# Attention and SoLU block on one core: the first two batches in slots of two pairs, v loaded once, q in halves

## The chip, the cores and the metric

The kernel runs on one core of a Trainium2 chip. Its engines are named as in the profile: PE (TensorE matmul) with PEld (its weight loads), DVE (VectorE), ACT (ScalarE), POOL (GpSimd) and SP (SyncE, which here only issues DMAs). The metric is the device time of one execution in microseconds (us); less is better.

## What is computed

The reference has two blocks. Batch is 8, heads 8, sequence 576, head width 64; the second block is 512 to 1024 to 512 wide.

```python
def _attn_ref(q, k, v, tau):
    scale = 1.0 / np.sqrt(q.shape[-1])
    scores = scale * np.matmul(q, k.transpose(0, 1, 3, 2))
    thresh = np.max(scores, axis=-1, keepdims=True) - tau
    scores = np.where(scores >= thresh, scores, -1000000000.0)
    scores = scores - np.max(scores, axis=-1, keepdims=True)
    attn = np.exp(scores)
    attn = attn / (np.sum(attn, axis=-1, keepdims=True) + 1e-09)
    return np.matmul(attn, v).astype(np.float32)

def _moe_ref(x, w_in, w_out, g_ln):
    h = x @ w_in
    h_max = np.max(h, axis=-1, keepdims=True)
    e = np.exp(h - h_max)
    sm = e / (np.sum(e, axis=-1, keepdims=True) + 1e-09)
    solu = h * sm
    mu = np.mean(solu, axis=-1, keepdims=True)
    var = np.mean((solu - mu) ** 2, axis=-1, keepdims=True)
    ln = (solu - mu) / np.sqrt(var + 1e-06) * g_ln
    return (ln @ w_out).astype(np.float32)
```

The heads of a token are laid side by side between the two blocks. All activations are float32. The weights `w_in`, `w_out` and `g_ln` come as float64, and the kernel converts them itself with integer operations on 16 pieces of 128 x 512, 512 KB each (`raw`).

## The kernel before

**Rounds.** The heads of a batch form four pairs. A slot is one step of attention for 128 queries: the scores against all 576 keys, for two heads side by side in two PSUM buffers (`s0`, `s1`). Two slots (r = 0 and 1) make a unit, and a unit is what one PV multiplication takes. Of a batch's 18 slots, kinds 0 and 1 have four units each (one for each pair), and kind 2 has the last 64 queries of all heads (the "ends"). The main loop runs 144 rounds, a slot in each. In a round: `scores` (L492, 16 matmul records on PE), the row maximum on DVE (`maxes`, L514), threshold and exponential on ACT (`ramp` L529, `exps` L538), then for the slot of the round before the division on POOL (`normalise`, L545 to L548) and a 32 x 32 block transpose on DVE (`blocks`, L559) into `T`. After a unit's second slot `spread` issues three DMAs on SP (L580, L582; L589 for ends), which put T's blocks in place in `wT`. When a unit's time has come (`pv_due`), `attend_steps` multiplies wT by v (L619, 72 matmuls) into a PSUM buffer `pv`, and `attended` has ACT copy it to `xh` or `xe` (L652), the input of the second block.

**Before round 30** (`START`) the kernel also fills itself: the pairs of batch 0 and 1 are loaded, turned and evicted, the weights are converted, and four blocks of the second block (`fronts`) are run at rounds that a table fixes: `ff_h` (L1041), a chain on DVE, ACT and POOL up to V (L1124) and its turn (L1157), `ff_o` (L1175) into PSUM `o_ps`, `ff_out` (ACT copies it to `ob`, L1195), `ff_store`. From round 30 on the matmuls of the second block go into two PSUM buffers that are held for good (`both["h"]`, `both["o"]`), and a PV shares the buffer of o. Before round 30 a PV takes one of two pair buffers (`p0`, `p1`) of its own.

**q, k and v of the first two batches.** `load_pair` (L132) brings the first 512 rows of two heads of q or k in one DMA of 256 KB; partition p gets the four rows 4p to 4p+3. `load_ends` (L143) brings the last 64 rows. PE turns them with matmuls against the identity (`turn`, L360), ACT and DVE copy the turned pieces out of PSUM into qT, kT and qe (`q_item` L396 and L400, `k_item` L420, `e_item` L435 and L439), either as `items` of a round's `scores` (batch 1, table PREP) or by `whole_pair`. Before the loop `turned` turns k of pair 0 and a quarter of its q; round 0 turns the other three quarters; whole pairs 1, 2 and 3 come at rounds 0, 2 and 4. A unit here is one pair with both slots, so v has to lie in two orders of its rows: `load_v` (L174, L179) loads, for half a batch (four heads), all 512 rows in 512 KB, then the same rows again with the two partition halves swapped in 2 x 256 KB, then the last 64 rows twice (2 x 64 KB).

**Queues.** SP's queue runs in order and carries the loads, the spreads, most raw pieces and the stores. The first three raw pieces (`weight_load`, L267) are issued by ACT's queue, as are k of pair 0 and tau. A piece goes to one of four work buffers (table RAW) and may be loaded when the piece before it in that buffer has been read. An instruction is issued in the order in which the program names it on its engine; what is not ready holds up all that is behind it on that engine.

**Tables.** PIECE says when each weight piece is loaded and converted (in quarters of a round), FETCH when a load of batch 1 and of v is issued, PREP when a piece of batch 1 is turned, HO in which rounds before 30 the four fronts are multiplied, LAG how much later than its least age a unit's PV is due. In `loose` rounds (19, 28, 29 here: no front, after round 16) DVE copies the scores out with the maximum, so that PSUM comes free earlier.

Of the kernel before, what the change touches and what calls it, by code (L numbers as in the profile page):

```python
# [8 lines left out]
F32 = mybir.dt.float32  # L9
# [11 lines left out]
def kernel(  # L21
# [35 lines left out]
    NB = S // 32  # L57
    SCALE = -0.125
# [67 lines left out]
    def load_pair(i, nm, queue=None):  # L126
        b, hp = divmod(i, NP)
        src = {"q": q, "k": k}[nm]
        raw = raw_tile(nm)[:, 0 : 8 * D].rearrange("p (h t d) -> p h t d", h=2, t=4)
        qk[nm, i] = raw  # L130
        queue = queue or nc.sync
        queue.dma_start(  # L132
            out=raw.rearrange("p h t d -> p h (t d)"),
            in_=src[b, 2 * hp : 2 * hp + 2, 0:SM, :].rearrange("h (p t) d -> p h (t d)", t=4),
        )
        if hp == 0:
            if b not in ends:
                ends[b] = loads.tile([P, H, D], F32, tag="ends", name="ends")
            load_ends(b, nm, slice(0, 2) if b == 0 else slice(0, H), queue)

    def load_ends(b, nm, of, queue):
# [3 lines left out]
        )  # L145

    def load_v(b, hf, parts=(0, 1, 2)):
# [19 lines left out]
        if 0 in parts:  # L167
            d["v"] = loads.tile([P, 4, NK, D], F32, tag="v", bufs=3, name="v")
# [47 lines left out]
    def constants():  # L216
# [4 lines left out]
        for g in range(2):  # L221
            of = 64 + 32 * (1 - g)
            nc.gpsimd.tensor_copy(
                out=swapped[ROWS[1], 32 * g : 32 * g + 32], in_=ident[ROWS[1], of : of + 32]
            )
# [33 lines left out]
    raws = {}  # L259

    def weight_load(x):
        raw = work.tile(
            [P, 512], I64 if wide else F32, tag=("u1", "u2", "uT", "xh1")[RAW[x]],
            bufs=1, name="raw"
        )
# [8 lines left out]

# [79 lines left out]
    def turn(spare, x, lhsT_of, swap=False):  # L354
# [3 lines left out]
        for r in range(2):  # L358
            for y in range(2):
                nc.tensor.matmul(  # L360
                    out=spare[r][ROWS[y], to], lhsT=lhsT_of(r, y),
                    rhs=swapped[ROWS[1]] if swap and r else ident[ROWS[r], ROWS[r]],
# [21 lines left out]
    def q_item(i, ts=slice(0, 4)):  # L384
        qT = pair(i)["qT"].rearrange("p (t r k) -> p r t k", t=4, r=2)
        n = ts.stop - ts.start

        def make(spare, x):
            for t in range(n):
                turn(  # L390
                    spare, x + t, lambda r, y: qk["q", i][ROWS[r], y, ts.start + t], swap=True
# [54 lines left out]
    def whole_pair(i):  # L446
        tags, tiles = zip(take("tp"), take("tp"))
        spare = dict(enumerate(tiles), base=0, eased=i > 0)
# [20 lines left out]

    def scores(s, items):  # L470
# [10 lines left out]
        for ks in (slice(SM, S), slice(0, SM)):  # L481
            for h in range(2):
                for y in range(2):
                    if kind < 2:
# [4 lines left out]
                    else:  # L489
                        d = pairs[b * NP + r + 2 * y]  # L490
# [100 lines left out]
    def attend_steps(key):  # L591
# [13 lines left out]
        for e in range(2) if kind == 2 else [None]:  # L605
            for m in range(NK):
                for u in range(2):
                    d, h0 = source(b * NP + (hp if e is None else e + 2 * u))
                    for h in range(2):
# [4 lines left out]
                        else:  # L614
# [8 lines left out]
                                m ^ 4 * u if m < 8 and b < 2 else m,  # L623
# [7 lines left out]
    def attended(key):  # L631
# [7 lines left out]
        if kind == 2:  # L639
            if b % 2 == 0:  # L640
                xe[b // 2] = work.tile([P, NP, P], F32, tag="xe", bufs=1, name="xe")
            to = xe[b // 2][:, :, 64 * (b % 2) : 64 * (b % 2) + 64].rearrange(
                "p (u r) y -> p u r y", u=2
# [939 lines left out]
```

## Time and profile before

| | us |
|---|---|
| three runs | 849.86, 847.30, 849.82 |
| median | 849.82 |
| the profiled execution | 846.98 |
| its span, first to last instruction | 845.0 |
| PE busy | 799.7 (95%) |
| DVE busy | 671.5 (79%) |
| ACT busy | 604.4 (72%) |
| POOL busy | 565.2 (67%) |
| mean granted clock of PE | 0.981 |

The span is 1.98 us shorter than the execution's own time: what lies around it is not seen in the trace. Busy shares are averages over the whole span. The page's row of the span in 40 slices (each digit is tenths of a slice of 21 us; a 9 is 90% or more) shows where the engines are not busy:

```profile
PE   4769899999899999999999999999999999999997
PEclk9679999999999999999999999999999999999999
DMA  7999688887877868887788768887788767555122
```

PE is under 80% busy in the first three slices (0 to 63 us) alone, the clock granted to it is low in the second and third, and the DMA engines are at 90% or more in slices two to four. The first two batches fill rounds 0 to 35; round 31 begins at 178.57 us.

### The profile page before, as it was taken

Reading aid. Unit: us, or ns where it says so; the run is one execution under the profiler, and the core shown is the slowest. Engines: PE = TensorE matmul, PEld = TensorE weight load, DVE = VectorE, ACT = ScalarE, POOL = GpSimd, SP = SyncE. Lnnn points to the kernel's source line nnn. Section 1 sums busy time; section 2 is a strip of 40 time slices with the busy share of each in tenths; the row PEclk is TensorE's granted clock in tenths of the full one; section 3 lists DMA queues with packets and bytes.
Section 4 is the critical chain, followed back from the end, with each engine's and each line's share of the span. In section 5 each row is a group of like instructions: output and inputs, shape, how many; then the busy total and the mean of one; then the engine's idle time right before and its main releaser. Section 6 shows DMA issues by size and latency. Waiting matters only on the chain.

```text
span 845.0 us, 36864 instructions
## 1 busy us (share of the span) xinstructions
PE 799.7 (95%) x15345; PEld 589.3 (70%) x15345; DVE 671.5 (79%) x1324; ACT 604.4 (72%) x1214; POOL 565.2 (67%) x1031
## 2 busy tenths in 40 slices
PE   4769899999899999999999999999999999999997
PEld 3435567767566886777776677767786677788786
DVE  3888968867889878888889888888888888787362
ACT  5979977676777777778787777878787687876231
POOL 3976867866757758585867758585867758574330
PEclk9679999999999999999999999999999999999999
DMA  7999688887877868887788768887788767555122
GB/s 231 272 231 259 181 221 225 213 220 191 222 224 208 228 149 240 229 216 207 204 244 223 204 163 246 225 221 196 216 238 218 207 159 211 144 152 137 37 62 52
DMA packets 100535, 167.44 MB, mean 198 GB/s; under 512 B 18248, under 2 KB 47952, under 8 KB 100368
## 3 DMA queue, kind: packets, MB, share of 16 engines
q1 hardware_dynamic: 99040, 162.82, 72.3%
q8 instruction: 121, 1.98, 1.0%
q10 hardware_dynamic: 1328, 2.26, 0.9%
q14 instruction: 46, 0.38, 0.1%
HBM read 46.14 MB, written 9.44 MB: 66 GB/s over the span
## 4 chain that ended last, share of the span: by engine, by line
PE 75%; ACT 7%; DMA 5%; POOL 4%; DVE 4%; issue 3%; SPq 2%; DVEq 0%; ACTq 0%; POOLq 0%
PE ov L1175 19%; PE h L735 16%; PE s_ps L492 14%; PE ov L619 12%; PE o_ps L1175 6%; PE h L759 4%; DMA wT<-T 3%; ACT w L529 2%; ACT w L538 2%; PE h_ps L1041 2%; DVE w L514 2%; PE pv L619 2%; POOL w L548 1%; DMA raw<-in_moe_w_out_dram 1%; DMA q<-in_q_dram 1%
## 5 line engine op out<-in xcount | busy, mean ns | idle before, releaser
L529 ACT ACTIVATE w<-s_ps,nth 128x576 f32<-128x576 f32 x282 | 199.6, 741 | 128.5 <-DVE nth L514 113.8
L514 DVE CUSTOM_DVE_ANT_0 w<-s_ps,tau_t 128x576 f32<-128x576 f32 x282 | 201.0, 749 | 55.0 <-PE s_ps L492 36.8
L548 POOL TENSOR_SCALAR w<-w,sm 128x576 f32<-128x576 f32 x288 | 219.0, 772 | 14.3
L559 DVE STREAM_TRANSPOSE T<-w 128x576 f32<-128x576 f32 x288 | 207.7, 756 | 17.8 <-POOL w L548 13.8
L538 ACT ACTIVATE w<-w,ntau 128x576 f32<-128x576 f32 x288 | 219.7, 768 | 0.0
L1175 PE MATMUL ov<-w,uT 64*64 64x256 f32 x3456 | 208.0, 376 | 0.7 <-issue 0.7
L492 PE MATMUL s_ps<-kT,qT 64*64 64x64 f32 (+1 forms) x2048 | 175.4, 424 | 15.1 <-ACT w L529 12.5
L619 PEld LDWEIGHTS ov<-wT,v 64*64 64x64 f32 x4752 | 150.6, 133 | 46.9 <-issue 33.6
L1175 PEld LDWEIGHTS ov<-w,uT 64*64 64x64 f32 x3456 | 160.6, 133 | 26.2 <-issue 1.2
L619 PE MATMUL ov<-wT,v 64*64 64x128 f32 (+1 forms) x4752 | 153.6, 259 | 1.2 <-DMA wT<-T 0.7
L545 POOL TENSOR_SCALAR sm<-sm 128x2 f32<-128x2 f32 x144 | 35.1, 244 | 143.5 <-ACT w L538 138.2
L546 POOL TENSOR_TENSOR sm<-sm,mone 128x2 f32<-128x2 f32 x144 | 104.1, 723 | 12.0
L735 PE MATMUL h<-w,xh 64*64 64x512 f32 x832 | 104.7, 591 | 0.6 <-POOL mark L110 0.4
L492 PEld LDWEIGHTS s_ps<-kT,qT 64*64 64x64 f32 x2048 | 71.4, 139 | 42.3 <-ACT w L529 19.1
L1175 PE MATMUL o_ps<-w,uT 64*64 64x256 f32 x1088 | 66.4, 377 | 0.7 <-ACT xh L652 0.5
L735 PEld LDWEIGHTS h<-w,xh 64*64 64x64 f32 x832 | 43.9, 133 | 31.4 <-issue 20.4
L1175 PEld LDWEIGHTS o_ps<-w,uT 64*64 64x64 f32 x1088 | 57.5, 133 | 10.8 <-issue 4.0
L1130 DVE TENSOR_SCALAR u<-u,rs,nb 128x1024 f32<-128x1024 f32 x32 | 28.8, 900 | 43.4 <-ACT V L1124 43.3
L1157 DVE STREAM_TRANSPOSE uT<-V 128x1024 f32<-128x1024 f32 x36 | 44.3, 1229 | 17.1 <-PE ov L1175 6.9
L538 ACT ACTIVATION_READ_ACCUMULATOR w<-w,ntau 128x1 f32 x288 | 55.7, 193 | 0.0
L735 PE MATMUL h<-k,sum 64*64 64x512 f32 x312 | 51.8, 589 | 0.0
L1124 ACT ACTIVATE V<-u,nb,rs 128x1024 f32<-128x1024 f32 x36 | 44.6, 1238 | 6.5 <-POOL nb L1102 6.4
(132 smaller groups left out, 1015.9 us busy)
## 6 DMA issues: line engine op xcount, KB each, us to landing
wT<-T SPq DMA_DIRECT2D x132, 288.0 KB, 4.5
wT<-T SPq DMA_DIRECT2D x256, 144.0 KB, 3.9
out_dram<-ob SPq DMA_DIRECT2D x71, 128.0 KB, 2.5
V<-u SPq DMA_DIRECT2D x136, 64.0 KB, 2.3
wT<-T SPq DMA_DIRECT2D x14, 576.0 KB, 6.4
q<-in_q_dram SPq DMA_DIRECT2D x24, 288.0 KB, 3.8
q<-in_k_dram SPq DMA_DIRECT2D x24, 288.0 KB, 4.3
v<-in_v_dram SPq DMA_DIRECT2D x12, 576.0 KB, 5.3
```

What stands on the lines that cost most here:

```text
L492: nc.tensor.matmul(out=ps[h][ROWS[y], ks], lhsT=lhsT, rhs=d["kT"][ROWS[h], ks], start=True, stop=True,)
L514: nc.vector.tensor_tensor_reduce(out=w, in0=ps[:, 0:S], in1=(zero if loose else tau_t).to_broadcast([P, S]), scale=1.0, scalar=BIG, op0=AL ...
L529: nc.scalar.activation(out=d["w"][x], in_=d["w"][x] if d["loose"] else d["ps"][x][:, 0:S], func=AF.Prelu, bias=d["nth"][x], scale=-1.0, al ...
L538: nc.scalar.activation(out=w, in_=w, func=AF.Exp, bias=ntau, scale=1.0, accum_out=sm[:, x : x + 1])
L546: nc.gpsimd.tensor_tensor(out=sm, in0=sm, in1=mone, op=ALU.pow)
L548: nc.gpsimd.tensor_scalar(out=w, in0=w, scalar1=sm[:, x : x + 1], scalar2=1.0, op0=ALU.mult, op1=ALU.mult)
L559: nc.vector.transpose(out=T[:, :, r, :, h, :], in_=w.rearrange("p (c m x) -> p c m x", c=2, x=32))
L619: nc.tensor.matmul(out=to, lhsT=d["v"][ROWS[u], (h0 + h - u) % 4 if b > 1 else h0 + h, m ^ 4 * u if m < 8 and b < 2 else m,], rhs=rhs, sta ...
L735: mm = nc.tensor.matmul(out=h[ROWS[y], 512 * bank : 512 * bank + 512], lhsT=x[ROWS[r], ROWS[y]], rhs=w[ROWS[r]], start=c == 0 and (n, r, k ...
L1124: nc.scalar.activation(out=V, in_=u, func=AF.Identity, bias=nb, scale=rs)
L1157: nc.vector.transpose(out=uT, in_=d["V"].rearrange("p y (m x) -> p m y x", x=32))
L1175: nc.tensor.matmul(out=to[ROWS[z], 0:256], lhsT=d["uT"][ROWS[r], m].rearrange("p y x -> p (y x)"), rhs=w2[ROWS[r], m ^ r, 256 * z : 256 * ...
```

## The change

Only the first two batches (`TILED` = 2) and the rounds before 30 are touched.

- **Slots of 64 queries of two pairs.** A slot takes 64 queries of each of two pairs instead of 128 queries of one. A unit is then a couple of pairs j (0: pairs 0 and 1; 1: pairs 2 and 3) and a half m of a kind's 256 queries; with MAJOR all 1 the order is (j, m) = (0,0), (0,1), (1,0), (1,1). Pairs 0 and 1 are both needed at round 0, pairs 2 and 3 at round 4 (before: pair 1 at round 2, pair 2 at 4, pair 3 at 6).
- **v once.** Each half of PE's rows takes another pair of heads, so one order of v is enough. Per half batch `load_v` issues four DMAs of 131 KB and two of 32 KB; one buffer holds a batch.
- **q in halves.** q of pairs 0 and 1 is loaded as two DMAs each (rows 4p, 4p+1 and 4p+2, 4p+3), the second ones behind the first raw piece. Before the loop k, a quarter of q and the ends of both pairs are turned (96 matmuls where 48 were); round 0 turns the second quarter of both, round 1 (LATE) the other half as items of its scores.
- **Whole pairs** 2 and 3 at rounds 1 and 3 (WHEN). The load of q of pair 3 moves from round 0 to the end of round 1.
- **Raw pieces.** The first three go over SP (QUEUE all 0). `weight_load` can put a piece into one of two v buffers (`stash`), for RAW values of 4 and more; the table RAW is as before.
- **o's buffer from round 17** (SHARE): `both["o"]` is taken at round 17, and a PV from there on goes into it, unless a front's o part stands in it unread. `ff_out` gives it back. PVs of the units that end with rounds 15, 17, 19, 21, 23, 25 run in rounds 18, 20, 22, 24, 27, 29 (before: 19, 20, 24, 25, 28, 29).
- PREP of one item of batch 1 moves from round 22 to 21; two more POOL copies fill the second half of `swapped` (the identity with its two 32-blocks exchanged), which q of odd pairs is turned with.

```diff
+    TILED = 2
...
+    def values(b, hf):
+        d = halves.setdefault((b, hf), {})
+        if "v" not in d:
+            if b < TILED:
+                both = loads.tile([P, 4, NK, D], F32, tag="v", bufs=3, name="v")
+                for x in range(2):
+                    halves[b, x] = dict(v=both[:, 2 * x : 2 * x + 2])
+            else:
+                d["v"] = loads.tile([P, 4, NK, D], F32, tag="v", bufs=3, name="v")
+        return halves[b, hf]["v"]
+
+    def stashed():
+        cols = 2 * NK * D if w_in.dtype == I64 else 4 * NK * D
+        return loads.tile([P, cols], w_in.dtype, tag="v", bufs=3, name="stash")
...
+        if b < TILED:
+            for u, rows in enumerate(ROWS):
+                of = v[b, 4 * hf + 2 * u : 4 * hf + 2 * u + 2]
+                to = d["v"][rows, 0:2].rearrange("p h m d -> p h (m d)")
+                for r in range(2) if 0 in parts else ():
+                    part = slice(256 * r, 256 * r + 256)
+                    nc.sync.dma_start(
+                        out=to[:, :, part],
+                        in_=of[:, part].rearrange("h (p t) d -> p h (t d)", t=4),
+                    )
+                if 2 in parts:
+                    nc.sync.dma_start(
+                        out=to[:, :, 512:], in_=of[:, SM:S].rearrange("h p d -> p h d")
+                    )
+            return
...
     def whole_pair(i):
         tags, tiles = zip(take("tp"), take("tp"))
-        spare = dict(enumerate(tiles), base=0, eased=i > 0)
+        spare = dict(enumerate(tiles), base=0, eased=bool(PAIRED[i]))
...
+    def unit_at(b, kind, n):
+        return divmod(n, 2) if MAJOR[2 * b + kind] else divmod(n, 2)[::-1]
...
-                    if kind < 2:
+                    if kind < 2 and b < TILED:
+                        j, m = unit_at(b, kind, hp)
+                        d = pairs[b * NP + 2 * j + y]
+                        t = P * (2 * kind + m) + 64 * r
+                        lhsT = d["qT"][ROWS[h], t : t + 64]
...
-    QUEUE = {0: 1, 1: 1, 2: 1, 3: 0, 4: 0, 5: 0, 6: 0, 7: 0, 8: 0, 9: 0, 10: 0, 11: 0, 12: 0, 13: 0, 14: 0, 15: 0}
...
+    LATE = {0: 1}
+    MAJOR = {0: 1, 1: 1, 2: 1, 3: 1}
+    PAIRED = {2: 1, 3: 1}
+    SHARE = {0: 17}
...
-    load_at = {}
+    load_at = {LATE[0]: [lambda: load_pair(3, "q")]}
...
+        stash = [stashed()]
+        values(0, 0)
+        stash.append(stashed())
+        load_pair(0, "q", ts=slice(0, 2))
+        load_pair(0, "k", nc.scalar)
         nc.scalar.dma_start(out=tau_t, in_=tau.partition_broadcast(P))
-        load_pair(0, "q")
-        load_pair(1, "q")
-        load_pair(0, "k", nc.scalar)
         load_pair(1, "k")
+        load_pair(1, "q", ts=slice(0, 2))
+        constants()
         weight_load(0)
-        constants()
+        for i in range(2):
+            load_pair(i, "q", ts=slice(2, 4))
         for x in range(1, 3):
             weight_load(x)
...
-        turned(first, [k_item(0), q_item(0, slice(0, 1)), e_item(0)])
-
-
-        whole = {0: 1, 2: 2, 4: 3}
...
+        turned(
+            first,
+            [k_item(0), q_item(0, slice(0, 1)), k_item(1), q_item(1, slice(0, 1)), e_item(0), e_item(1)],
+        )
...
             if rnd == START:
-                both["h"], both["o"] = take("h2")[1], take("ov")[1]
+                both["h"] = take("h2")[1]
                 oq.extend(t for x, t in enumerate(fronts) if HO.get(4 * x + 2, START) >= START)
+            if rnd == SHARE[0]:
+                both["o"] = take("ov")[1]
...
-                if due and "o" not in what and len(pairs_free) > ("h" in what and steps[0][1] == 0):
+                opened = both.get("open")
+                for kind, part, _ in steps:
+                    if kind == "o":
+                        opened = None if part else "fresh"
+                if due and opened != "used" and (
+                    "o" in both or len(pairs_free) > ("h" in "".join(x for x, _, _ in steps) and steps[0][1] == 0)
+                ):
```

163 lines of the change are left out of this document (119 added, 44 removed).

## The prediction

> **What bounds the kernel now.** I read the stretches of the span first, because the change touches only the first two batches (36 of 144 rounds) and an average over the span hides them. The columns are the stretch, its length, then busy time and instructions of PE, PEld, DVE, ACT and POOL, the granted clock of PE, the share of the DMA engines, GB/s.
>
> ```profile
> 0.00:18.00 18.00, 8.81 (x176) 5.55 (x176) 5.17 (x17) 7.74 (x20) 3.58 (x16) 1.00 0.81 249
> 18.00:70.00 52.00, 34.69 (x591) 22.57 (x595) 42.41 (x83) 41.87 (x92) 40.02 (x52) 0.74 0.99 240
> 50.00:60.00 10.00, 3.36 (x20) 1.11 (x20) 6.87 (x15) 7.96 (x18) 8.19 (x13) 0.60 1.05 234
> 70.00:104.00 34.00, 30.03 (x592) 20.54 (x584) 30.80 (x60) 32.25 (x69) 29.53 (x42) 1.00 0.82 222
> 104.00:176.00 72.00, 65.84 (x1381) 49.46 (x1381) 55.99 (x109) 51.74 (x112) 55.40 (x94) 0.98 0.86 219
> 176.00:845.00 669.00, 660.37 (x12620) 491.19 (x12612) 537.17 (x1060) 470.78 (x924) 436.67 (x830) 1.00 0.71 190
> ```
>
> From 176 us (round 31) on, PE is busy 660.37 of 669 us, and there the changed program issues the same instructions in the same order: nothing can be won or lost. From 18 to 70 us the DMA engines are full (0.99) and everything else has gaps; from 70 to 176 us PE is close to full (30.03 of 34, 65.84 of 72). So the question is what the change does to 18 to 70 us, and what of it reaches round 31.
>
> What the full DMA engines carry there, and how long one transfer needs from issue to landing (size, median us), against the median of the span in the last row:
>
> ```profile
> wT<-T SPq DMA_DIRECT2D x9, 288.0 KB, 10.3
> ...
> v<-in_v_dram SPq DMA_DIRECT2D x2, 512.0 KB
> v<-in_v_dram SPq DMA_DIRECT2D x4, 256.0 KB, 10.1
> v<-in_v_dram SPq DMA_DIRECT2D x4, 64.0 KB, 9.7
> q<-in_q_dram SPq DMA_DIRECT2D x1, 256.0 KB, 10.8
> ...
> wT<-T SPq DMA_DIRECT2D x132, 288.0 KB, 4.5
> ```
>
> Where it hurts is seen in ACT's waits of 20 to 70 us (the first row) and in the timeline (start, length, what; in brackets the idle time before and what ended it):
>
> ```profile
> ACT xh L652 <- PE pv L619: 5.0, 1, 5.0
> ...
> 43.07 1.42 ACT L529 ACTIVATE w<-s_ps,nth 128x576 f32<-128x576 f32 x2 [1.90 <-DVE nth L514]
> 56.41 1.42 ACT L529 ACTIVATE w<-s_ps,nth 128x576 f32<-128x576 f32 x2 [1.17 <-DVE nth L514]
> 60.18 3.89 PE L619 MATMUL pv<-wT,v 64*64 64x128 f32 x66 [0.45 <-DMA wT<-T]
> 60.26 1.44 DVE L559 STREAM_TRANSPOSE T<-w 128x576 f32<-128x576 f32 x2 [3.26 <-DMA wT<-T]
> 64.33 0.37 ACT L652 COPY xh<-pv 128x256 f32<-128x256 f32 x1 [4.99 <-PE pv L619]
> 66.75 1.42 ACT L529 ACTIVATE w<-s_ps,nth 128x576 f32<-128x576 f32 x2 [0.94 <-DVE nth L514]
> ```
>
> The third unit's spread wT came late, so PV started at 60.18 us, at half clock (3.89 us), and ACT, whose queue runs in order, stood 4.99 us before the copy of that PV and 0.94 us before the next ramp: round 10 starts 5.93 us later than ACT's own work asks.
>
> **The change, part by part.** *The start.* Before, ACT's queue is held by the issues of two raw pieces, and its share of the first evictions follows them; DVE begins its share at 7.13 us.
>
> ```profile
> 5.38 3.60 ACTq L267 DMA_DIRECT2D raw<-in_moe_w_in_dram  x2
> 5.49 1.13 PE L360 MATMUL tp<-ident,k 64*64 64x64 f32 x32 [5.49 <-DMA k<-in_k_dram]
> 7.13 0.42 DVE L420 COPY kT<-tp 128x256 f32<-128x256 f32 x1 [2.20 <-PE tp L360]
> 9.03 0.37 ACT L420 COPY kT<-tp 128x256 f32<-128x256 f32 x1 [4.38 <-DMA q<-in_q_dram]
> 9.50 0.32 ACT L435 ACTIVATE qe<-tp,scl 128x64 f32<-128x64 f32 x1
> 9.67 2.20 PE L492 MATMUL s_ps<-kT,qT 64*64 64x64 f32 x16 [2.62 <-ACT qT L396]
> ```
>
> With the raw pieces on SP, ACT is free at 7.1 us, about 2 us earlier. But round 0 now needs two pairs: 96 transposes for 48 (the second row's 32 of k, and 16 of q and ends), which at 1.13 us for 32 is 1.7 us more of PE, six evictions for three (ACT's three ran 9.03 to 9.82, so 0.8 us more), and pair 1's k must have landed. That is -2 + 1.7 + 0.8, less some overlap: +0.3 us; bounds -1 (transposes under the transfers) and +2.5 (no overlap at all).
>
> *Rounds 1 to 5.* One whole pair's evictions cost ACT 1.7 us:
>
> ```profile
> 24.99 0.82 ACT L396 ACTIVATE qT<-tp,scl 128x256 f32<-128x256 f32 x2
> 25.70 0.64 ACT L420 COPY kT<-tp 128x256 f32<-128x256 f32 x2
> 26.22 0.35 ACT L435 ACTIVATE qe<-tp,scl 128x64 f32<-128x64 f32 x1
> 26.43 0.24 ACT L439 COPY kT<-tp 128x64 f32<-128x64 f32 x1
> ```
>
> By round 4 there were three (pairs 1, 2, 3), now two: -1.7. Four evictions of the late q halves stand between round 1's ramps: each half the 0.82/2 row and its fixed part, +1.1 together; their 32 transposes stand ahead of round 1's scores, +1.3 with the wait behind them. Round 4 now needs pair 3, which is turned in round 3 and was needed only in round 6: its scores wait for ACT's 1.7 us, +1.8. With the start, 0.3 - 1.7 + 1.1 + 1.3 + 1.8 = +2.8 us at round 5. In rounds 6 to 9 ACT waits for DVE's maximum anyway (1.90 us before the ramp at 43.07, 1.17 before the one at 56.41, 3.1 together); I let half of the 2.8 vanish there: +1.4; bounds 0 (the 3.1 take it all) and +2.8.
>
> *v loaded once.* The three v rows are 2 x 512 + 4 x 256 + 4 x 64 KB, 2.36 MB; now half, 1.18 MB. In a full stretch at 240 GB/s that frees 4.9 us of transfer ahead of the wT at 60 us. The wait it feeds is 5.93 us. The next limit is DVE, which has weight steps to do before round 10's maximum; I leave 1.4 us of idle: -4.5. Bounds: -5.9 and 0.
>
> Against this part speaks a rule of the Trainium skill ("DMA: Bandwidth & Descriptors", section Bandwidth): batch transfers, since those under 64 KB are dominated by their descriptors, and 64 KB ran at 138 GB/s there. v now comes in 131 and 32 KB pieces. Worked out with that figure as an estimate, 1.18 MB would take 8.6 us against 9.8 for the 2.36 MB at 240 GB/s, and the part would be worth -1.2 in place of -4.9. The rows lean neither way: 64 KB landed in 9.7 us and 256 KB in 10.1, which in a full queue is mostly waiting in line. The trace cannot settle it; the third rival carries it.
>
> *PV in o's buffer from round 17.* The PV of the eighth unit runs one round earlier, in round 18, and its copy stands in ACT's order ahead of what follows here:
>
> ```profile
> 114.78 1.24 ACT L1124 ACTIVATE V<-u,nb,rs 128x1024 f32<-128x1024 f32 x1 [1.15 <-POOL nb L1102]
> 114.88 2.15 PE L619 MATMUL pv<-wT,v 64*64 64x128 f32 x72
> 115.93 0.57 ACT L1195 COPY ob<-o_ps 128x512 f32<-128x512 f32 x1
> 116.39 0.77 ACT L420 COPY kT<-s_ps 128x192 f32<-128x192 f32 x4
> 116.86 0.76 DVE L514 CUSTOM_DVE_ANT_0 w<-s_ps,zero 128x576 f32<-128x576 f32 x1 [2.85 <-ACT kT L420]
> ```
>
> DVE already waits 2.85 us for that kT. PV and its copy push it by 2.15 + 0.37, less the 1.15 that V waits for POOL anyway: +1.3; bounds 0 and +2.5. Up to round 28 the rounds carry one PV more than before (2.15 us in a PE-bound stretch), and later ones carry it less. A wait there gives some of it back:
>
> ```profile
> 169.86 0.56 ACT L1195 COPY ob<-o_ps 128x512 f32<-128x512 f32 x1
> 170.48 3.21 PE L619 MATMUL pv<-wT,v 64*64 64x128 f32 x72 [2.88 <-ACT ob L1195]
> ```
>
> The 2.88 us before round 29's PV stays, since that PV still follows ACT's ob in the same buffer; I count half of the 2.15 as returned: +1.0; bounds -1 and +2.2.
>
> *Second batch's v.* Another 1.18 MB less, while the DMA share is 0.86 and PE is busy 65.84 of 72 us: -1.0; bounds -2.5 and 0.
>
> *The rest at nothing.* Two POOL copies at the start lie in POOL's wait for the first raw piece. Of the two v buffers held for raw pieces, no piece is sent there by the table of buffers, whose values all stay below 4; so this part does nothing, and if it had been meant to relieve something, nothing of that comes.
>
> Sum: +1.4 - 4.5 + 1.3 + 1.0 - 1.0 = -1.8 us. The profiled run took 846.98 us (span 845.0), so its own time becomes 845.2; the median shown is 849.82, 2.8 above the profiled run, so the forecast is 848.0.
>
> **The rivals.** *First: more is won.* The lag of the first rounds is swallowed wholly (ACT's 3.1 us of waits are enough for 2.8), the PV moved forward finds the gaps that 65.84 of 72 leaves, and the second batch's relief is 1.5: 0 - 4.5 + 0 - 1.5 = -6.0, 843.8. For it: each swallowing has a row that is long enough. Against: three must hold together.
>
> *Second, slower: q of pair 3 comes late.* Its load moves from round 0 to the end of round 1, and on SP it is now queued behind raw pieces, the six v transfers and the wait below.
>
> ```profile
> SPq L267 <- ACT w L294: 4.2, 1, 4.2
> ...
> 21.98 0.55 SPq L267 DMA_DIRECT2D raw<-in_moe_w_in_dram  x1
> 28.37 0.48 PE L492 MATMUL s_ps<-kT,qT 64*64 64x64 f32 x4 [1.53 <-ACT w L529]
> ```
>
> Before, SP reached this place at about 22 us. With the 10.8 us of the q row it lands at 32.8; round 4's scores stood at 28.4: +4.4. PE takes in order, so round 3's transposes block round 4, and the lag then is too long for rounds 6 to 9 (another +1.4): -1.8 + 4.4 + 1.4 = +4.0, 853.8. It decides from a landing of some 6.4 us on; the sign of the whole turns at about 8. Against: where the engines are not full, 288 KB land in 4.5 us (the last row of the transfers), and half of v is gone from the queue.
>
> *Third: nothing is freed.* If in this stretch time goes by the number of transfers and not by their bytes (the 9.7 and 10.1 us above), twelve v transfers for ten free nothing, the -4.5 falls away, and the sum is +2.7: 852.5. Against: 240 GB/s at a share of 0.99 looks like bytes. This is the rule quoted above in its sharpest form.
>
> **How the numbers follow.** Forecast 0.40, first rival 0.28, second 0.24, third 0.08. A measurement of this kernel can tell 0.3%, 2.55 us, from no change. The forecast's own spread is 3 us either way (845 to 851): 0.16 faster, 0.19 same, 0.05 slower. The first rival is faster but for 0.01; the second slower but for 0.04; the third half and half. Together 0.43 faster, 0.28 same, 0.29 slower. The range runs from the first rival with another 2.8 (the rest of the 5.9 and of the second relief), 841, to the second with 2.2 (PV's whole upper bound), 856.
>
> **What would show it.** v's landing and the wT before the third unit's PV: ACT's 4.99 before xh falls under 2, and the clock of 50 to 60 us rises above 0.60. Round 9's first ramp, at 56.41 before, stands some 1.4 us later; a PE wait for q's transfer in round 3 or 4 means the second rival. DVE's 2.85 before round 19's maximum grows by about 1.3. The stretch up to 176 us carries the whole difference: if the later 669 us also change, the reasoning is wrong, and so it is if the DMA share of 18 to 70 us stays 0.99 with the same end.

## The result, and the profile after

The changed kernel is slower: 853.9 us median against 849.91 us for the kernel before (22 runs each), ratio 1.0046 with the interval 1.0026 to 1.0065, so 2.2 to 5.5 us. That is on the other side of zero from the forecast of 848.0, though inside its range of 841 to 856. Its profiled run, 860.97 us (span 859.0), happens to be the slowest of its 22, so most readings below have a second profile of each kernel beside them.

The stretches of the changed kernel, with the columns of the prediction:

```profile
0.00:18.00 18.00, 7.94 (x172) 6.10 (x176) 5.11 (x17) 6.80 (x19) 2.29 (x16) 1.00 0.77 234
18.00:70.00 52.00, 34.83 (x581) 23.74 (x577) 43.24 (x83) 42.79 (x95) 43.04 (x57) 0.73 0.87 216
50.00:60.00 10.00, 6.67 (x145) 4.87 (x141) 9.46 (x20) 9.11 (x20) 8.86 (x12) 0.93 0.87 222
70.00:104.00 34.00, 31.18 (x578) 21.92 (x574) 28.72 (x58) 30.72 (x64) 26.59 (x39) 0.92 0.85 219
104.00:176.00 72.00, 63.71 (x1326) 46.88 (x1316) 55.43 (x107) 50.60 (x111) 51.46 (x87) 0.97 0.76 189
176.00:845.00 669.00, 658.97 (x12540) 509.40 (x12544) 537.95 (x1063) 473.45 (x930) 442.10 (x837) 1.00 0.71 191
```

The DMA engines did get free: 0.87 for 0.99 in 18 to 70 us, and the clock of 50 to 60 us rose from 0.60 to 0.93 (in the second profiles 0.85 for 1.01, and from 0.67 to 0.79). But PE did no more in 18 to 70 us than before (34.83 for 34.69 us; 34.72 for 35.69 in the second profiles), and less in 104 to 176 (63.71 for 65.84; 65.78 for 66.08). The bytes went and the time did not.

Where it went is read from the start of ACT's first ramp in each round, which the timeline gives. The table has the lengths between them, in us; "rest" runs from round 30 to the last one, 143. One profile is left out, the first of the kernel of the last row, since its execution (854.88 us) was a slow one, over 1.5% above the fastest of its kernel.

| kernel | round 0 at | 0 to 9 | 9 to 12 | 12 to 18 | 18 to 30 | round 30 at | rest |
|---|---|---|---|---|---|---|---|
| before | 13.2 | 43.3 | 19.5 | 34.6 | 65.8 | 176.3 | 594.1 |
| before, again | 12.9 | 43.3 | 16.4 | 35.6 | 66.5 | 174.5 | 596.2 |
| changed | 15.0 | 45.6 | 17.1 | 35.0 | 70.3 | 183.0 | 600.5 |
| changed, again | 15.2 | 45.5 | 15.4 | 35.6 | 68.5 | 180.1 | 599.4 |
| PVs late | 13.9 | 45.6 | 15.5 | 33.7 | 70.5 | 179.1 | 603.0 |
| v twice | 16.2 | 46.1 | 16.4 | 33.8 | 70.0 | 182.4 | 596.7 |
| o's buffer at 30 | 15.1 | 45.8 | 17.9 | 34.9 | 64.8 | 178.5 | 598.7 |
| PVs mixed | 16.3 | 45.3 | 13.9 | 36.6 | 67.4 | 179.3 | 597.9 |
| pair 3 early | 15.3 | 44.5 | 13.8 | 35.4 | 68.3 | 177.3 | 596.4 |
| raw in v buffers | 14.2 | 45.4 | 15.4 | 35.3 | 69.2 | 179.4 | 598.7 |
| before, o's buffer at 17 | 14.0 | 43.5 | 16.6 | 34.9 | 69.9 | 178.9 | 598.0 |
| k first | 12.5 | 45.6 | 16.3 | 34.5 | 67.2 | 176.1 | 597.8 |
| o at 30, pair 3 early | 14.2 | 44.6 | 16.7 | 33.8 | 66.1 | 175.3 | 592.8 |
| and k first | 12.6 | 44.3 | 14.1 | 33.8 | 66.5 | 171.3 | 596.9 |
| and raw, again | 12.5 | 44.4 | 13.9 | 34.3 | 64.6 | 169.7 | 595.1 |

Round 30 stands 6.1 us later on the mean of two profiles each (181.5 against 175.4). Behind it the same instructions took 592.8 to 603.0 us from one execution to the next, so a single profile's end tells little. The first 30 rounds tell more, and there the loss lies in three places.

*Round 0 and rounds 1 to 9.* The timeline of the changed kernel:

```profile
8.14 1.13 PE L402 MATMUL tp<-ident,k 64*64 64x64 f32 x32 [2.48 <-DMA k<-in_k_dram]
14.97 1.39 ACT L580 ACTIVATE w<-s_ps,nth 128x576 f32<-128x576 f32 x2
...
30.48 1.42 ACT L580 ACTIVATE w<-s_ps,nth 128x576 f32<-128x576 f32 x2 [0.99 <-DVE nth L565]
33.32 0.82 ACT L439 ACTIVATE qT<-tp,scl 128x256 f32<-128x256 f32 x2
34.76 0.24 ACT L482 COPY kT<-tp 128x64 f32<-128x64 f32 x1
35.15 2.20 PE L543 MATMUL s_ps<-kT,qT 64*64 64x64 f32 x16
38.29 1.42 ACT L580 ACTIVATE w<-s_ps,nth 128x576 f32<-128x576 f32 x2 [2.15 <-DVE nth L565]
...
47.13 1.42 ACT L580 ACTIVATE w<-s_ps,nth 128x576 f32<-128x576 f32 x2 [0.43 <-DVE nth L565]
...
60.54 1.42 ACT L580 ACTIVATE w<-s_ps,nth 128x576 f32<-128x576 f32 x2 [1.19 <-DVE nth L565]
```

PE stands 2.48 us for k of pair 1 before it can turn it; round 0's ramp is 1.8 us late. In round 4 everything is in series: ACT copies pair 3 (33.32 to 35.0), then PE computes the scores at half clock (2.20 us at a granted clock of 0.50; it was 0.50 for round 4's scores before too), then DVE's maximum, and ACT has waited 2.15 us by the ramp. Round 3 to round 4 takes 7.8 us (30.48 to 38.29), before 4.6. By round 5 the lag is 5.5 us. Round 5 to round 6 then takes 4.5 us, before 5.9, and ACT's wait before round 6's ramp is 0.43 us (47.13) for 1.90: 1.5 us are won back there. Behind round 6 nothing is: 4.1 us are left at round 9 (60.54 against 56.41).

*Rounds 9 to 12.* The longest wait for wT is now that of the next PV, at 65.51 us (one row for the first four matmuls, one for the rest):

```profile
64.94 1.42 ACT L580 ACTIVATE w<-s_ps,nth 128x576 f32<-128x576 f32 x2
65.51 0.69 PE L673 MATMUL pv<-wT,v 64*64 64x128 f32 x4 [2.25 <-DMA wT<-T]
66.56 3.89 PE L673 MATMUL pv<-wT,v 64*64 64x128 f32 x66 [0.36 <-DMA wT<-T]
70.71 0.37 ACT L710 COPY xh<-pv 128x256 f32<-128x256 f32 x1 [2.84 <-PE pv L673]
73.02 1.42 ACT L580 ACTIVATE w<-s_ps,nth 128x576 f32<-128x576 f32 x2 [0.19 <-DVE nth L565]
```

ACT's wait before the copy is 2.84 us for 4.99, and a round later. Against the first profile of the kernel before, round 10 gains 5.9 us on the lag of round 9, and round 11 gives 3.1 of them back.

*Rounds 18 to 30.* The PV that moved to round 18:

```profile
116.27 2.15 PE L673 MATMUL ov<-wT,v 64*64 64x128 f32 x72
118.48 0.37 ACT L710 COPY xh<-ov 128x256 f32<-128x256 f32 x1 [2.74 <-PE ov L673]
118.75 1.24 ACT L1224 ACTIVATE V<-u,nb,rs 128x1024 f32<-128x1024 f32 x1
120.98 0.77 ACT L463 COPY kT<-s_ps 128x192 f32<-128x192 f32 x4 [0.52 <-PE s_ps L543]
121.45 0.76 DVE L565 CUSTOM_DVE_ANT_0 w<-s_ps,zero 128x576 f32<-128x576 f32 x1 [5.34 <-ACT kT L463]
```

ACT waits 2.74 us for the PV with V, ob and kT behind it, and DVE's maximum now waits 5.34 us for kT where it waited 2.85 (in the second profiles 3.62 for 2.86).

### The profile page after: what moved, and what is told of

It reads as the page before. It is cut to its first block, busy times and chain, and to the rows that moved or that the text cites. A ratio compares the mean times of both kernels' runs of the same rounds, so it can differ in the third digit from the quotient of the medians.

```text
span 859.0 us, 36874 instructions
## 1 busy us (share of the span) xinstructions
PE 806.3 (94%) x15345; PEld 615.8 (72%) x15345; DVE 672.1 (78%) x1327; ACT 605.3 (70%) x1217; POOL 565.6 (66%) x1033
## 4 chain that ended last, share of the span: by engine, by line
PE 74%; DMA 7%; ACT 5%; DVE 4%; issue 3%; POOL 3%; SPq 2%; DVEq 0%; ACTq 0%; POOLq 0%
PE ov L1275 19%; PE s_ps L543 15%; PE h L793 14%; PE ov L673 13%; PE o_ps L1275 5%; DMA wT<-T 5%; PE h L817 4%; ACT w L580 2%; PE h_ps L1141 2%; DVE w L565 1%; DVE T L610 1%; ACT w L589 1%; POOL w L599 1%; DMA V<-u 1%; DMA k<-in_k_dram 1%
## 5 line engine op out<-in xcount | busy, mean ns | idle before, releaser
L1275 PE MATMUL ov<-w,uT 64*64 64x256 f32 x3840 | 233.4, 376 | 2.5 <-issue 1.1
L673 PEld LDWEIGHTS ov<-wT,v 64*64 64x64 f32 x5256 | 172.4, 134 | 52.7 <-issue 34.4
L1275 PEld LDWEIGHTS ov<-w,uT 64*64 64x64 f32 x3840 | 186.3, 133 | 28.2 <-issue 3.5
L543 PE MATMUL s_ps<-kT,qT 64*64 64x512 f32 (+1 forms) x2048 | 180.2, 426 | 16.6 <-ACT w L580 13.0
L673 PE MATMUL ov<-wT,v 64*64 64x128 f32 (+1 forms) x5256 | 173.8, 260 | 9.0 <-DMA wT<-T 6.0
L543 PEld LDWEIGHTS s_ps<-kT,qT 64*64 64x64 f32 x2048 | 77.2, 140 | 43.1 <-ACT w L580 20.0
L793 PE MATMUL h<-w,xh 64*64 64x512 f32 x832 | 107.0, 591 | 0.6 <-POOL mark L111 0.4
L793 PEld LDWEIGHTS h<-w,xh 64*64 64x64 f32 x832 | 48.2, 133 | 28.7 <-issue 16.4
L1257 DVE STREAM_TRANSPOSE uT<-V 128x1024 f32<-128x1024 f32 x36 | 44.2, 1227 | 15.5 <-PE ov L1275 7.5
L1224 ACT ACTIVATE V<-u,nb,rs 128x1024 f32<-128x1024 f32 x36 | 44.6, 1239 | 6.8 <-POOL nb L1202 6.7
L839 DVE CUSTOM_DVE_ANT_0 u<-h,u 128x512 f32<-128x512 f32 x52 | 35.0, 676 | 14.5 <-PE h L793 13.6
L1187 DVE BATCH_NORM_STATS2 bs<-u 128x6 f32<-128x512 f32 x72 | 45.5, 674 | 0.1
```

The costliest lines, as they stand in the source:

```text
L543: nc.tensor.matmul(out=ps[h][ROWS[y], ks], lhsT=lhsT, rhs=d["kT"][ROWS[h], ks], start=True, stop=True,)
L673: nc.tensor.matmul(out=to, lhsT=d["v"][ROWS[u], (h0 + h - u) % 4 if b > 1 else h0 + h, m ^ 4 * u if m < 8 and TILED <= b < 2 else m,], rhs ...
L793: mm = nc.tensor.matmul(out=h[ROWS[y], 512 * bank : 512 * bank + 512], lhsT=x[ROWS[r], ROWS[y]], rhs=w[ROWS[r]], start=c == 0 and (n, r, k ...
L1187: nc.vector.bn_stats(out=bs[:, f], in_=u[:, 512 * f : 512 * f + 512])
L1224: nc.scalar.activation(out=V, in_=u, func=AF.Identity, bias=nb, scale=rs)
L1275: nc.tensor.matmul(out=to[ROWS[z], 0:256], lhsT=d["uT"][ROWS[r], m].rearrange("p y x -> p (y x)"), rhs=w2[ROWS[r], m ^ r, 256 * z : 256 * ...
```

## The experiments

**The kernel before once more**, without an edit.

> The kernel before, unchanged, profiled once more, to see how far two profiles of one kernel differ. If the loss is made in the first 30 rounds (my theory), round 30's first ramp stands at 176.3 us here as before, within 1 us, and executions differ only behind it. Rival: the first rounds differ from execution to execution by as much as the two kernels do (6 us).

It took 847.41 us. Round 9 is as in the first profile (56.12), but the wait that the prediction was built on is not there:

```profile
57.52 1.44 DVE L559 STREAM_TRANSPOSE T<-w 128x576 f32<-128x576 f32 x2 [0.81 <-DMA wT<-T]
61.01 0.37 ACT L652 COPY xh<-pv 128x256 f32<-128x256 f32 x1 [1.96 <-PE pv L619]
62.69 1.42 ACT L529 ACTIVATE w<-s_ps,nth 128x576 f32<-128x576 f32 x2 [0.17 <-DVE nth L514]
```

ACT stood 1.96 and 0.17 us in place of 4.99 and 0.94, with a DMA share of 1.01 in 18 to 70 us. Two executions of one kernel differ by 3.2 us in rounds 9 to 12. Round 30 stands 1.8 us earlier than in the first profile (174.5 for 176.3): more than the 1 us of the theory, far less than the 6 of the rival.

**The changed kernel once more**, without an edit.

> The changed kernel, unchanged, profiled once more. Its first profile led (stood later than before) by 1.8 us at round 0, 4.1 at round 9, 1.3 at round 11, 2.1 at round 18, 6.7 at round 30 and 13.1 at the end. Theory: the leads up to round 30 are seen again within 1 us, and what comes behind round 30 is chance, so the end stands 4 to 8 us later than in the kernel before. Rival: the lead grows by another 5 us or more behind round 30 again, and the loss is in the steady rounds, through other addresses or other phases of the queues.

It took 856.84 us. A lead is how much later than in the first profile of the kernel before a ramp stands. Up to round 9 the leads agree within 0.25 us, as the theory says; from round 11 on they are smaller by more than its 1 us (0.1 us at round 12 for 1.7, 3.7 at round 30 for 6.7). From round 30 to the last one it took 599.4 us, 5.3 more than the first profile of the kernel before, as the rival says, but only 3.2 more than the second. That is settled neither way by these four.

**PVs put back to the rounds of before, o's buffer still from round 17.**

```diff
-    LAG = {1: 2, 3: 1, 5: 1, 9: 1, 11: 1, 17: 0, 21: 0, 23: 1, 25: 1}
+    LAG = {1: 2, 3: 1, 5: 1, 9: 1, 11: 1, 15: 1, 17: 0, 19: 2, 21: 1, 23: 2, 25: 1}
```

> The changed kernel with the PVs of rounds 18 to 29 put back to the rounds of before (19, 20, 24, 25, 28, 29); o's buffer is still taken from round 17 on. Theory: the lead at round 18 (2.1 us) stays as it is and the 4.5 us that rounds 18 to 30 add fall away, lead at round 30 some 2 us, time near 850. Rival: it is the shared buffer and not the round that costs, then the lead at round 30 stays above 5 us and the time at 854.

857.22 us, ratio 1.0091 (1.0058 to 1.0124): no better than the change itself (1.0026 to 1.0065). Rounds 18 to 28 took 56.4 us, as before (56.5 and 57.1; the changed kernel 60.1 and 58.2), so the PVs' places do cost what the theory says there. Then the step from round 28 to 29 takes 11.0 us for 3.8, 7.1 more, which nobody expected; the next step gives 2.4 back (3.1 us for 5.5):

```profile
168.49 4.12 PE L673 MATMUL ov<-wT,v 64*64 64x128 f32 x72 [5.94 <-ACT ob L1297]
172.67 0.37 ACT L710 COPY xh<-ov 128x256 f32<-128x256 f32 x1 [4.24 <-PE ov L673]
173.98 2.14 PE L673 MATMUL ov<-wT,v 64*64 64x128 f32 x72
174.19 0.76 DVE L565 CUSTOM_DVE_ANT_0 w<-s_ps,zero 128x576 f32<-128x576 f32 x1 [7.05 <-PE s_ps L543]
```

The PV of round 28 finds o's buffer occupied by a front's result until ACT has copied it to ob (5.94 us), and after that idle time PE runs it at half clock (4.12 us at a granted clock of 0.50, against 2.14 for the next). The shared buffer has a price of its own when a PV falls just behind an o part. So each of the two explanations holds for a part of the stretch. The lead at round 30, 2.8 us, looks like the theory's 2, but this execution began earlier (round 0 at 13.9 us for 15.0 and 15.2); rounds 18 to 30 took 70.5 us in all, no less than in the change.

**v's bytes loaded twice**, the second time into a buffer that nothing reads.

```diff
+            if b == 0:
+                again = stash[1].bitcast(F32)[:, 0 : 4 * NK * D].rearrange(
+                    "p (h n) -> p h n", h=4
+                )
+                if 0 in parts:
+                    nc.sync.dma_start(
+                        out=again[:, :, 0:256],
+                        in_=v[b, hs, 0:SM, :].rearrange("h (p t) d -> p h (t d)", t=4),
+                    )
+                if 2 in parts:
+                    nc.sync.dma_start(
+                        out=again[ROWS[0], :, 256:320],
+                        in_=v[b, hs, SM:S, :].rearrange("h p d -> p h d"),
+                    )
```

> The changed kernel with 1.18 MB of batch 0's v loaded a second time, into a buffer that nothing reads, beside the first: the bytes of before. Theory: the stretch of 18 to 70 us is bound by bytes, the wait of some 5 us in rounds 9 to 11 comes back, the lead at round 12 rises from 1.7 to 5 us or more, time 856 to 858. Rival: v's bytes were hidden anyway, the lead at round 12 stays under 2.5 us and the time at 854.

852.95 us, ratio 1.0051 (1.0021 to 1.0081), the same as the changed kernel. Of the views of 18 to 70 us, the second transfers and the stretch:

```profile
stash<-in_v_dram SPq DMA_DIRECT2D x2, 512.0 KB, 8.0
stash<-in_v_dram SPq DMA_DIRECT2D x2, 64.0 KB, 6.5
...
18.00:70.00 52.00, 36.39 (x580) 22.59 (x577) 42.90 (x84) 44.34 (x99) 40.66 (x54) 0.66 0.92 236
```

The bytes are back (236 GB/s for 216) and rounds 9 to 12 take 16.4 us, between the changed kernel's two profiles (17.1, 15.4). The lead at round 12 reads 2.6 us, between the two expectations, but it was 5.8 at round 9 already, from a late start: the stretch that the bytes should have lengthened is not longer, and the wait of some 5 us is not back (ACT waits 2.5 us for that PV, between the 2.8 and 1.8 of the changed kernel's profiles). The rival holds in what it says of v's bytes: in this kernel they are hidden, as far as one profile and a time known to 0.3% can tell.

**o's buffer from round 30 again**, with the rest of the change.

```diff
-    SHARE = {0: 17}
+    SHARE = {0: 30}
...
-                if due and opened != "used" and (
+                if due and (opened != "used" if "o" in both else "o" not in what) and (
```

> The changed kernel with o's buffer taken at round 30 as before: PVs before it in buffers of their own, in the rounds of before. From round 18's ramp to round 30's the kernel before took 65.8 and 66.5 us in its two profiles, the changed kernel 70.3 and 68.5. Theory: the PVs moved forward cost this, so the stretch takes about 66 us again and the time falls by 2 to 4 us to 850 to 852. Rival: it is the new slots that make the stretch longer (the PV in two-pair slots waits for other things), then it stays at 68 or more and the time at 854.

850.96 us, ratio 1.0008 (0.9969 to 1.0047). Rounds 18 to 30 took 64.8 us, even less than in the kernel before (the later versions with this edit: 64.6 to 66.5). The theory holds for the stretch; the time's interval still touches that of the change.

**Three PVs put back, two left.**

```diff
-    LAG = {1: 2, 3: 1, 5: 1, 9: 1, 11: 1, 17: 0, 21: 0, 23: 1, 25: 1}
+    LAG = {1: 2, 3: 1, 5: 1, 9: 1, 11: 1, 15: 1, 17: 0, 19: 2, 21: 1, 23: 1, 25: 1}
```

> The changed kernel with only the PVs of rounds 18, 22 and 24 put back to 19, 24 and 25; those of rounds 27 and 29 stay, in o's buffer. Theory: the 7 us that round 29 lost with all of them put back do not appear, and rounds 18 to 30 take some 67 us, time about 851. Rival: any PV moved back in the shared buffer meets o's parts later, and the stretch takes 70 us or more.

853.11 us, ratio 1.0032 (0.9999 to 1.0065); rounds 18 to 30 took 67.4 us, as the theory says, and round 29 lost nothing. The time does not tell it from the change.

**Pair 3 turned in round 2.**

```diff
     WHEN = {
         2: 1,
-        3: 3,
+        3: 2,
     }
...
-    load_at = {LATE[0]: [lambda: load_pair(3, "q")]}
+    load_at = {}
```

with the load of its q back in round 0.

> The changed kernel with pair 3 turned in round 2 and not 3, and the load of its q back in round 0. Theory: round 4's scores no longer wait for pair 3's copies (ACT stood 2.15 us there), so the step from round 3's ramp to round 4's falls from 7.8 to about 5.5 us; but round 3 has the copies then, so the lead at round 9 falls only by 1 to 2 us, from 4.2 to about 2.7, and the time by as much. Rival: ACT's copies are the whole of it and only change places, the lead at round 9 stays at 4.2.

```profile
31.32 1.43 ACT L580 ACTIVATE w<-s_ps,nth 128x576 f32<-128x576 f32 x2
35.74 1.42 ACT L580 ACTIVATE w<-s_ps,nth 128x576 f32<-128x576 f32 x2 [0.39 <-DVE nth L565]
```

Round 3 to 4 fell to 4.4 us (7.8), more than expected, and the lead at round 9 to 3.4, less than expected: round 6 takes back what rounds 4 and 5 had won. The time, 853.31 us (1.005, 1.0021 to 1.0078), shows no difference.

**The raw pieces in the v buffers.**

```diff
-    RAW = {0: 0, 1: 1, 2: 2, 3: 3, 4: 0, 5: 1, 6: 2, 7: 3, 8: 0, 9: 1, 10: 2, 11: 3, 12: 0, 13: 1, 14: 2, 15: 0}
+    RAW = {0: 0, 1: 1, 2: 2, 3: 3, 4: 4, 5: 5, 6: 0, 7: 1, 8: 2, 9: 3, 10: 4, 11: 5, 12: 0, 13: 1, 14: 2, 15: 0}
```

> The changed kernel with the fifth and sixth raw piece sent to the two v buffers that it holds for them and does not use (and the later ones spread over all six). SP no longer waits 6.8 us at 12 us for a buffer, so v, the next raw pieces and q of pair 3 are issued earlier. Theory: the first nine rounds are bound by ACT and DVE and not by transfers, so round 9 moves by under 0.5 us; rounds 9 to 12, which took 15.4 to 17.1 us, fall by 1 at most; the time falls by 1 at most. Rival: the transfers bind after all and this part was where the gain lay, then the time falls by 3 or more.

852.69 us, ratio 1.0044 (1.0009 to 1.0079): nothing, as the theory said. Its rounds 9 to 12 (15.4 us) are those of the changed kernel.

**The kernel before with o's buffer from round 17**, the rest as it was.

```diff
-                both["h"], both["o"] = take("h2")[1], take("ov")[1]
+                both["h"] = take("h2")[1]
...
+            if rnd == 17:
+                both["o"] = take("ov")[1]
...
-                if due and "o" not in what and len(pairs_free) > ("h" in what and steps[0][1] == 0):
+                if due and opened != "used" and (
+                    "o" in both or len(pairs_free) > ("h" in "".join(x for x, _, _ in steps) and steps[0][1] == 0)
+                ):
```

> The kernel before with one part of the change alone: o's buffer is taken at round 17 and the PVs from there on go into it, so those of rounds 19, 24, 25 and 28 come earlier. Round 18's ramp to round 30's took 65.8 and 66.5 us in its profiles. Theory: the PVs moved forward cost by themselves, so this takes 68 us or more and the time rises by 2 to 4 us. Rival: the cost needs the two-pair slots, then it stays at 66 and the time at 849 to 850.

853.03 us, ratio 1.0064 (1.0033 to 1.0094). This part alone loses as much as the whole change. Its timeline has the same two places as the changed kernel:

```profile
112.39 2.15 PE L619 MATMUL ov<-wT,v 64*64 64x128 f32 x72
114.60 0.37 ACT L652 COPY xh<-ov 128x256 f32<-128x256 f32 x1 [2.53 <-PE ov L619]
116.90 0.77 ACT L420 COPY kT<-s_ps 128x192 f32<-128x192 f32 x4 [0.32 <-PE s_ps L492]
117.37 0.76 DVE L514 CUSTOM_DVE_ANT_0 w<-s_ps,zero 128x576 f32<-128x576 f32 x1 [4.93 <-ACT kT L420]
...
137.12 2.23 PE L619 MATMUL ov<-wT,v 64*64 64x128 f32 x72
140.86 0.76 DVE L514 CUSTOM_DVE_ANT_0 w<-s_ps,tau_t 128x576 f32<-128x576 f32 x1 [2.56 <-PE s_ps L492]
141.72 1.42 ACT L529 ACTIVATE w<-s_ps,nth 128x576 f32<-128x576 f32 x2 [1.94 <-DVE nth L514]
```

The first is the kT that follows the PV's copy on ACT (2.85 us of DVE's wait before, 4.93 now). The second is the PV of round 22, 2.23 us of PE ahead of round 23's scores, which DVE waits for. Rounds 18 to 30 take 69.9 us for 65.8 and 66.5.

**k of pair 1 first on SP's queue**, ahead of q, and the first raw piece behind the second q halves.

```diff
+        load_pair(1, "k")
-        load_pair(0, "q", ts=slice(0, 2))
         load_pair(0, "k", nc.scalar)
         nc.scalar.dma_start(out=tau_t, in_=tau.partition_broadcast(P))
-        load_pair(1, "k")
+        load_pair(0, "q", ts=slice(0, 2))
         load_pair(1, "q", ts=slice(0, 2))
         constants()
-        weight_load(0)
         for i in range(2):
             load_pair(i, "q", ts=slice(2, 4))
+        weight_load(0)
```

> The changed kernel with k of pair 1 first on SP's queue, and the first raw piece behind the second q halves. Theory: round 0 is late because the transposes wait 2.48 us for k of pair 1, which lands at 8.1 us; earlier, it lets round 0's ramp start at 13.5 us or before (15.0 and 15.2 in the changed kernel, 13.2 and 12.9 before), and the lead at round 9 falls by as much. Rival: twice the copies set round 0, and it stays at 14.7 or later.

```profile
5.72 1.11 PE L402 MATMUL tp<-ident,k 64*64 64x64 f32 x32
...
12.52 1.39 ACT L580 ACTIVATE w<-s_ps,nth 128x576 f32<-128x576 f32 x2
```

PE turns k of pair 1 at 5.72 us without a wait (8.14 before), round 0's ramp starts at 12.52 us, and the lead at round 9 is 1.7 us for 4.1 and 4.3. The one execution took 851.25 us. The late start was the order of the first transfers and not the copies. The edit moves the raw piece as well as k, and tau lands earlier too (DVE's first use of it is at 6.21 us for 7.91), so k's own share is not shown apart.

**o's buffer at 30 and pair 3 early**, by the two edits above.

> The changed kernel with both parts undone that cost by themselves: o's buffer at round 30, pair 3 turned in round 2 with its q loaded in round 0. Theory: the gains add (64.8 us for rounds 18 to 30 instead of 68.5 to 70.3, round 9 at 59.8 instead of 60.6), the time is 849 to 851, the same as before within 0.3%. Rival: the stretch of rounds 9 to 12 gives the start's gain back, and it stands at 851 to 853.

850.06 us, ratio 1.0022 (0.9996 to 1.0048), as expected; round 30 at 175.3 us.

**The same, with k first and the raw pieces in the v buffers.**

> The same with k of pair 1 first on SP's queue and the fifth and sixth raw piece in the v buffers besides. Theory: round 0 at 13.5 us, round 9 under 58.5, rounds 9 to 12 in 14 to 15.5 us (16.4 to 19.5 before), rounds 18 to 30 in 65, so round 30 at 174 to 175 us (176.3 and 174.5 before) and the time 847 to 849: it would be as fast as the kernel before or up to 0.3% faster. Rival: the start cannot be had, and it stands at 850 to 852.

846.94 us, ratio 0.9986 (0.9952 to 1.0019), just under what was expected; round 0 at 12.8 us, round 9 at 57.3.

**The same without the raw pieces, and with them once more.**

> The changed kernel with o's buffer at round 30, pair 3 turned in round 2 and k of pair 1 first, but no raw piece in the v buffers. Theory: without the raw pieces spread over six buffers, rounds 12 to 18 take some 34 us as in the other kernels (38.5 with them in one profile), and rounds 9 to 12 are 1 to 2 us longer than with them: round 30 at 173 to 175 us, the time 846 to 849, 0 to 0.3% faster than the kernel before. Rival: the v buffers carried the gain of the version with all four, then the time is that of the version without k first, 850.

> The version with all four once more, beside it on one chip. Theory: its 846.9 of the first time are seen again, 0.9975 to 1.0 of the kernel before; its rounds 12 to 18, 38.5 us in a profile of a disturbed execution, take 34 to 36. Rival: those 38.5 us belong to the six buffers and are seen again.

847.78 us, ratio 0.9976 (0.995 to 1.0001), and 848.73 us, ratio 0.9983 (0.9956 to 1.0011). Rounds 12 to 18 took 33.8 and 34.3 us, so the 38.5 were that one execution's; the raw pieces add nothing. Round 30's ramp in the first of the two:

```profile
171.33 1.42 ACT L580 ACTIVATE w<-s_ps,nth 128x576 f32<-128x576 f32 x2 [2.47 <-POOL sum L769]
```

Round 30 stands 3 to 7 us earlier than in the kernel before (171.3 and 169.7 against 174.5 and 176.3). The medians of all three runs of these versions lie 1 to 2 us under the kernel before, and none of the three intervals excludes no change.

## Why the prediction was wrong

**v loaded once, -4.5 us: the step that failed.** The forecast was right about the DMA engines (share 0.99 to 0.87) and wrong about the cost that it hung on them. The size was taken from one wait of one execution: 5.93 us of ACT at round 10. The second profile of the kernel before has 2.1 us there, and the kernel before with o's buffer from round 17, whose first rounds are the same, 3.2. Nor was the whole of it a wait for wT that the profile shows. This row of the kernel before stands ahead of the one at 60.18:

```profile
59.04 0.69 PE L619 MATMUL pv<-wT,v 64*64 64x128 f32 x4 [3.64 <-issue]
```

For its 3.64 us of idle PE the profile names nothing that ended them; only the 0.45 us behind it are put down to the transfer. On the mean of two profiles each, rounds 9 to 12 take 16.2 us for 17.9, a gain of 1.7. The spread is larger: the five profiles whose first twelve rounds are the changed kernel's lie between 13.9 and 17.9 us, the three of the kernel before's between 16.4 and 19.5. v's bytes brought back leave the stretch at 16.4. So the first profile's wait was the largest of several that vary, and no price. The wait that was left also went on to the next PV instead of ending, as the row at 65.51 us shows. Two signs of the forecast came true all the same (ACT no longer waits before the third unit's copy, and the clock of 50 to 60 us rose), and the time did not follow them.

**Rounds 1 to 9, +1.4 us: the second step that failed.** The terms up to round 5 were mis-sized (+2.8 forecast, 5.5 and 5.7 measured). The start was off by 1.5 us (+0.3 forecast, 1.8 measured): round 0 stands at 12.5 to 12.8 us in every kernel with k first and at 13.9 to 16.3 in the others with the new slots, so it is the order of the transfers and not the copies. Round 4 was off by 1.4 us (+1.8 forecast, 3.2 measured): copies, scores and maximum stand there in series. The other terms, +0.7 together, came to 0.5. Half of the lag was then to vanish in ACT's two waits for DVE, 1.4 us, and 1.5 us did, all of it at the first, before round 6. The second, 1.17 us before round 9, is 1.19 in the changed kernel and took nothing; rounds 6 to 9 take 13.3 us before (43.07 to 56.41) and 13.4 after. So the part that the waits swallow had the right size by luck, and what came into it was twice the forecast. 4.1 and 4.3 us were left.

**PV in o's buffer, +2.3 us: right in mechanism, mis-sized.** The part alone costs 3.8 us in rounds 18 to 30 (69.9 against a mean of 66.1), and 1.0064 in the time. Step by step, from one round's ramp to the next, the profiles of the table part by where the PVs stand, whatever the slots (us; the kernel with three PVs put back is in the left column for the first three steps and in the right one for the last):

| step | PVs in their old rounds | PVs moved forward |
|---|---|---|
| 18 to 19 | 8.1 | 8.8 to 10.5 |
| 22 to 23 | 3.9 to 4.2 | 5.8 to 6.5 |
| 25 to 27 | 10.8 | 8.9 to 9.0 |
| 27 to 28 | 6.1 | 7.4 to 8.2 |

The place in round 18 was the one named (kT behind the PV's copy). What had been counted as one PV more, half returned, is a PV ahead of the scores of rounds 23 and 28 (before round 23's it keeps PE 2.23 us, and DVE and then ACT wait, as the rows of that part alone show), less the 1.9 us that rounds 25 to 27 return. That round 29's wait for ob stays was right, but the PV behind it took 4.12 us for 3.21:

```profile
176.23 4.12 PE L673 MATMUL ov<-wT,v 64*64 64x128 f32 x72 [2.78 <-ACT ob L1297]
```

The late PVs showed how much larger that wait can be. The rule of the Trainium skill that fits this ("TensorE: Matmul & The Clock Gate", Part 1: after an idle window of some 3.4 us PE falls to half clock) agrees with the row at 168.49: 5.94 us idle, then 4.12 us for a PV that takes 2.14. The row at 176.23 shows the same 4.12 us behind only 2.78 us without any work.

**The second batch's v, -1.0 us.** Not seen apart. With o's buffer at round 30 the stretch of rounds 18 to 30 takes 64.8, 66.1, 66.5 and 64.6 us for 65.8 and 66.5 before, a mean of 65.5 for 66.1; a gain of that size is within the spread.

**The sum.** On the mean of two profiles each, the measured terms are 4.3 us for the first nine rounds, -1.7 for rounds 9 to 12, 0.2 for 12 to 18 and 3.3 for 18 to 30 (69.4 against 66.1): 6.1 us, as much as round 30 stands later. The time grew by 2.2 to 5.5. That the steady rounds issue the same instructions was right, but they vary by 10 us, more than everything forecast. Two sums of the stated range do not come out: the rests of the 5.9 and of the second relief are 1.4 and 1.0, 2.4 and not 2.8, and of PV's upper bound of 2.2 the second rival already holds 1.0.

**The rivals.** *q of pair 3 late* came nearest in its time (853.8 against 853.9), and that was luck, for what it describes did not come about. Its sign did show, a PE wait for that q in round 3, but only of 0.7 us, as the waits of 20 to 75 us have it, and the turned pieces then stood ready before ACT could copy them at 33.32. Its place, round 4, did lose 3.2 us; the loss there was the serial chain that the forecast had as a term.

```profile
PEld tp L402 <- DMA q<-in_q_dram: 0.7, 1, 0.7
```

*Nothing is freed* was near in its time too (852.5), but for another reason: bytes were freed, and little waited for them. The transfers of 18 to 70 us in the changed kernel (size, median us to landing):

```profile
v<-in_v_dram SPq DMA_DIRECT2D x8, 128.0 KB, 5.4
v<-in_v_dram SPq DMA_DIRECT2D x4, 32.0 KB, 5.5
```

The rule of the Trainium skill on small transfers that was weighed beside this rival ("DMA: Bandwidth & Descriptors", section Bandwidth) shows no price here: the pieces land in little more than half the time that the larger ones took before (10.1 and 9.7 us), at a DMA share of 0.87 for 0.99. At what rate each size would run alone, no run shows. *More is won* needed three gains together, and none came whole. That the two v buffers are not used and cost nothing by it was right.

## What to carry to other kernels

A wait in one profile is a sample: before a forecast is built on one stall in a stage with full DMA engines, see it in a second profile of the same kernel. Whether a wait is slack for a lag made earlier is not seen from its length: of two waits counted here, 1.90 us took 1.5 us of the lag and 1.17 us took none. Compare how long the rounds take. Work moved forward on an engine that runs in order is paid by what is queued behind it there: here PVs moved forward cost 3.8 us, while 1.18 MB less to load gave some 1.7 us, less than the spread.

## What was not expected of the hardware

The 113 rounds from 30 on, the same instructions in the same order, took 592.8 to 603.0 us in the profiles shown here. A part of it is waits of PE for wT, spread over the span: the waits of 176 to 844 us (total, times, longest) have nine in the first profile of the changed kernel, then four in the second profile of the kernel before (the other two profiles of these kernels have eight of 4.3 us in all, and two of 0.7):

```profile
PE ov L673 <- DMA wT<-T: 6.0, 9, 1.4
```

```profile
PE ov L619 <- DMA wT<-T: 2.7, 4, 1.3
```

Whether the changed kernels have more of them by more than chance is left open: the twelve profiles with its slots average 597.8 us there, the three with the slots of before 596.1.
